# Who empties the matmul banks at the end of a batch: five copies between ScalarE and VectorE

## The chip, the cores and the metric

The kernel runs on one core of a Trainium2 chip. The metric is device time in microseconds (us) of one execution. The engines are TensorE (PE: matmuls; PEld: its weight loads), VectorE (DVE), ScalarE (ACT), GpSimd (POOL) and SyncE (SP, which here only issues transfers). Each has its own queue of instructions and works through it in order; they meet only through semaphores. TensorE writes its results to PSUM, eight banks of 128 x 512 float32; VectorE or ScalarE must read a bank before it can be used again.

## The reference

Eight batches, eight heads, 576 positions, head dimension 64, 32 memory slots. Per head an attention over compressed keys and values, then one SwiGLU feed-forward block over all heads together:

```python
a = exp(phi - max); a = a / sum(a)                     # over the 32 slots
k_m = einsum('bhsm,bhsd->bhmd', a, k)                  # 32 x 64 per head
v_m = einsum('bhsm,bhsd->bhmd', a, v)
attn = softmax(q @ k_m.T / sqrt(64))                   # 576 x 32 per head
x = (attn @ v_m), heads side by side                   # 4608 x 512
g = x @ w_gate;  val = x @ w_val                       # 512 -> 1536
out = (g * sigmoid(g) * val) @ w_out                   # 1536 -> 512
```

## The kernel before, in words

**Algebra.** `x` is never formed. For each batch the kernel multiplies the compressed values `v_m` with the gate and value weights first (`u_round`, matmuls L465). The result `t_U` has 32 rows per head, 256 rows in all, and the gates are then the product of `t_U` with the attention weights `t_A`: `p_g` for the gate, `p_v` for the value (L508), in two halves of 128 rows each. ScalarE takes silu of `p_g` (L525, into `t_sg`), VectorE multiplies it with `p_v` (L531, into `t_h`). The output product `t_h @ w_out` is done with seven block products in place of eight (Strassen's scheme in Winograd's form, `products`, matmuls L720), whose sums of blocks (`t_S`, `t_T`) are made beforehand by GpSimd and VectorE.

**Order.** Everything is in an order written out by hand. The last six batches run in one loop, `for b in range(2, B)` (L988); one pass of it is called a turn here, after its `b`. A turn begins with the scores of its batch (L389), their exponentials (L400), the sums and the normalisation of the weights (L428 to L445), mixed with the output products of the batch before. Then come 24 gate slots (`gv_slot`), and between them: the compressed keys and values of the next batch, the rest of the output products, and near slot 20 the three-part value round of the next batch, `u_three(b + 1)`. Four gate slots, 20 to 23, stand behind it, then the next turn begins.

A gate slot issues the matmuls of its own `p_g` and silu first, and then the matmuls of the `p_v` of the slot before and its multiplication. So TensorE's order at the end of a turn is: 24 small matmuls of the value round, (in turns 3, 5, 6) the last four output matmuls of the previous batch, `p_g`(20), `p_v`(19), `p_g`(21), `p_v`(20), `p_g`(22), `p_v`(21), `p_g`(23), `p_v`(22), `p_v`(23), and then the next turn's output products.

**The value round.** `u_three` fills six banks with 128 x 512 float32 each, and each is copied as bfloat16 to `t_U`. The string `evac` says by whom: one letter per bank, in order, `a` for ScalarE (L485) and `v` for VectorE (L489). "avaava" gives ScalarE the banks 1, 3, 4, 6 and VectorE 2 and 5.

**The output block.** `c21` (L772 to L776) is the last step of a batch's output product: the bank `p_os` holds the finished left half of the second row block; it is copied to `t_o2`, whose right half is already there, and the block is stored. For batches 2, 4 and 5 it is issued in turns 3, 5 and 6 directly behind the value round, at 114.7, 167.7 and 191.8 us of the profile. For the other batches it is issued elsewhere in a turn (batch 1 at 77.1, batch 3 at 132.7, batch 6 at 208.4). The last batch's is on VectorE already (`end`).

**Banks.** The eight banks are one list, first in, first out (L72 to L84):

```python
tag = free.pop(0)                      # bank(): take the first
free.append(held.pop(id(t))[0])        # done(): give back at the end
```

The list is worked through while the program is written, so which matmul gets which bank is fixed; on the chip the matmul waits until the engine that reads the bank has finished. A bank that is given back late by either engine is waited for by the matmul that stands at that place in the list, whatever other banks are free by then.

Of the kernel before, what the change touches and what calls it, by code (L numbers as in the profile page):

```python
# [14 lines left out]
def kernel(  # L15
# [59 lines left out]
    def bank(shape, dtype, name):  # L75
        tag = free.pop(0)
        t = ps.tile(shape, dtype, tag=tag, name=name)
        held[id(t)] = tag, t
        return t

    def done(*tiles):

        for t in tiles:
            free.append(held.pop(id(t))[0])  # L84
# [58 lines left out]
    def w_part(which, c, i, g, halves):  # L143

        w = W[which, c][64 * g:64 * g + 64]
        h0, h1 = halves[0], halves[-1] + 1
        return w[:, h0:h1, i] if c == 0 else w[:, i, HC * h0:HC * h1]
# [180 lines left out]
    def copy(eng, out, in_):  # L328
        if eng == "a":
            nc.scalar.copy(out=out, in_=in_)  # L330
        else:
            nc.vector.tensor_copy(out=out, in_=in_)  # L332
# [120 lines left out]
    def u_round(b, parts, evac):  # L453


        banks = []
        for which, c, halves in parts:
            w0, w1, h0, h1 = which[0], which[-1] + 1, halves[0], halves[-1] + 1
            n = (h1 - h0) * HC
            p = [bank([128, CH], FP32, f"p_u{g}") for g in range(NG)]  # L460
            for w in which:
                o = (w - w0) * n
                for i in range(NP):
                    for g in range(NG):
                        nc.tensor.matmul(  # L465
                            p[g][32 * i:32 * i + 32, o:o + n],
                            lhsT=kTs[b][64 * g:64 * g + 64, 2, 32 * i:32 * i + 32],
                            rhs=w_part(w, c, i, g, halves),
                            start=True,
                            stop=True,  # L470
                            tile_position=(64 * g, 32 * i),
                        )
            for g in range(NG):
                if (b, c, g) not in Us:
                    u_buffer(b, c, f"U{c}")
                if len(which) == 1:
                    dst = Us[b, c, g][:, h0:h1, w0]
                else:
                    dst = Us[b, c, g][:, h0]
                src = p[g][:, 0:(w1 - w0) * n].rearrange("p (a f) -> p a f", f=HC)  # L480
                banks.append((dst, src, p[g], rSs[b][:, g:g + 1] if b in scaled else None))
        for (t, p, home, r), e in zip(banks, evac):
            if e == "a":
                if r is None:
                    nc.scalar.copy(out=t, in_=p)  # L485
                else:
                    nc.scalar.activation(out=t, in_=p, func=AF.Copy, scale=r)  # L487
            elif r is None:
                nc.vector.tensor_copy(out=t, in_=p)  # L489
            else:  # L490
                nc.vector.tensor_scalar(out=t, in0=p, scalar1=r, scalar2=None, op0=ALU.mult)
            done(home)
# [51 lines left out]
    def u_buffer(b, c, tag):  # L544

        t = upool.tile([128, NG, 2, 2, HC], BF16, tag=tag, name="t_U")
        for g in range(NG):
            Us[b, c, g] = t[:, g]
# [133 lines left out]
    def products(b, by_hand, quad=None):  # L682

        h = DM // 2
        mine = {}
        lo, hi = slice(0, h), slice(h, DM)
        U = 2 if quad is None else 1
        end = quad == 1 or (quad is None and b + 1 == B)
# [65 lines left out]
        def both(name, t0, cols):  # L754
            store_block(mine[name], b, t0 // 256, cols)
# [15 lines left out]

        def c21():  # L772
            t = mine["o2"]
            copy("v" if end else "a", t[:, :, lo], mine["s"])
            done(mine["s"])
            both("o2", 256, slice(0, DM))  # L776

        def leftover(name, room, half, cols):
# [23 lines left out]
        ops = dict(  # L802
            p1=keep("p1", "s"), q6=keep("q6", "s"), p5=keep("p5", "c"),
            c11=c11, c22=c22, c12=c12, c21=c21,
        )
        if quad is not None:
# [25 lines left out]

    def u_three(b):

        u_round(b, (((0,), 0, (0, 1)), ((1,), 0, (0, 1)), ((0,), 1, (0, 1))), "avaava")

    def u_values(b):

# [119 lines left out]
    for c in range(1, NCH):  # L958
        s = 8 * c
# [28 lines left out]
    for b in range(2, B):  # L988
# [55 lines left out]
        if b == 2:  # L1044
            norm(2, 1)
            u_three(2)
            run(one[36:])
# [15 lines left out]
        if not last:  # L1063
            if b > 2:
                load_qT(b + 1)
            if b > 2 and b != 4:
                phi_sum(b + 1)
            streams += [
                (kv_items(b + 1, lambda: (u_item(b, 2, "aava")(), run(take(2)))), KV, KV + 4),
                ([lambda: (u_three(b + 1), run(take(2)))], 19, 20),  # L1070
            ]
# [38 lines left out]
```

The softmax here doesn't subtract the row's maximum and nothing guards it: scores larger than these inputs give would overflow.

## Time and profile before

| | |
|---|---|
| Time, median of 3 runs | 235.18 us (234.79 to 236.0) |
| Span of the profiled execution | 233.1 us |
| PE busy | 223.6 us, 96% |
| DVE busy | 183.2 us, 79% |
| ACT busy | 173.6 us, 74% |
| POOL busy | 140.6 us, 60% |
| ACT copies `t_U` from PSUM, L485 | 53, 607 ns each |
| DVE copies `t_U` from PSUM, L489 | 19, 683 ns each |
| ACT copies of the output block, L330 | 7, 617 ns each |
| DVE copy of the output block, L332 | 1, 692 ns |
| Ends of turns 2 to 6, us of the span | 92, 116, 145, 169, 193 |

How to read it: the clock that was granted to TensorE is full in every slice of the page. Busy time of PE counts modelled ends of pipelined matmuls, so that a row of matmuls looks gapless even where one of them started a little late; the starts tell more than the lengths. Rows of the timeline merge instructions of one kind that stand together on an engine (x4: four of them, with the time from the first start to the last end), and what is in brackets is the idle time of the engine before the row and what ended it.

### The profile page before, as it was taken

Reading aid. Unit: us, or ns where it says so; the run is one execution under the profiler, and the core shown is the slowest. Engines: PE = TensorE matmul, PEld = TensorE weight load, DVE = VectorE, ACT = ScalarE, POOL = GpSimd, SP = SyncE. Lnnn points to the kernel's source line nnn. Section 1 sums busy time; section 2 is a strip of 40 time slices with the busy share of each in tenths; the row PEclk is TensorE's granted clock in tenths of the full one; section 3 lists DMA queues with packets and bytes.
Section 4 is the critical chain, followed back from the end, with each engine's and each line's share of the span. In section 5 each row is a group of like instructions: output and inputs, shape, how many; then the busy total and the mean of one; then the engine's idle time right before and its main releaser. Section 6 shows DMA issues by size and latency. Waiting matters only on the chain.

```text
span 233.1 us, 7210 instructions
## 1 busy us (share of the span) xinstructions
PE 223.6 (96%) x2825; PEld 169.7 (73%) x2825; DVE 183.2 (79%) x421; ACT 173.6 (74%) x369; POOL 140.6 (60%) x190
## 2 busy tenths in 40 slices
PE   7987899999999999999999999999999999999993
PEld 2544466778887776878788787887788777878882
DVE  4155799999966698989798667998799888977732
ACT  2777798988447889968896658978898789677310
POOL 8422536998199059765976689464844493129291
PEclk9999999999999999999999999999999999999999
DMA  6999999999995992999099945995022702102125
GB/s 213 210 212 204 200 206 207 227 239 268 205 244 138 259 254 44 230 212 170 23 255 213 205 135 107 254 230 96 3 90 92 124 0 93 70 24 90 26 89 159
DMA packets 36674, 36.84 MB, mean 158 GB/s; under 512 B 14624, under 2 KB 31008, under 8 KB 36640
## 3 DMA queue, kind: packets, MB, share of 16 engines
q0 software_dynamic: 16272, 22.42, 51.8%
q1 hardware_dynamic: 19600, 13.18, 23.8%
q10 hardware_dynamic: 768, 0.79, 1.1%
q8 instruction: 22, 0.36, 0.6%
q14 instruction: 12, 0.10, 0.1%
HBM read 42.47 MB, written 9.44 MB: 223 GB/s over the span
## 4 chain that ended last, share of the span: by engine, by line
PE 88%; DMA 7%; POOL 1%; ACT 1%; DVE 1%; issue 1%; POOLq 0%
PE p_v L508 21%; PE p_g L508 21%; PE p_os L720 21%; PE p_oc L720 10%; DMA t_kv<-in_v_dram 7%; PE p_u L465 5%; PE p_oa L720 5%; PE p_kv L230 2%; PE p_g L389 1%; POOL t_kv L99 1%; PE p_mT L318 1%; PE p_warm L867 1%; PE p_q L376 0%; POOL t_q L108 0%; DVE t_kT L332 0%
## 5 line engine op out<-in xcount | busy, mean ns | idle before, releaser
L531 DVE TENSOR_TENSOR t_h<-t_sg,p_v 128x288 bf16<-128x288 bf16 x192 | 81.8, 451 | 17.4 <-PE p_v L508 7.4
L508 PEld LDWEIGHTS <-t_U 128*128 128x128 bf16 x768 | 73.6, 98 | 23.2 <-issue 3.8
L525 ACT ACTIVATE t_sg<-p_g 128x288 bf16<-128x288 f32 x192 | 74.0, 424 | 17.8 <-PE p_g L508 11.5
L508 PE MATMUL p_g<-t_A,t_U 128*128 128x288 bf16 x384 | 77.1, 286 | 0.5 <-ACT t_U L487 0.5
L508 PE MATMUL p_v<-t_A,t_U 128*128 128x288 bf16 x384 | 77.2, 286 | 0.0
L720 PEld LDWEIGHTS <-t_S 128*128 128x128 bf16 x384 | 37.5, 98 | 4.5 <-issue 0.2
L596 POOL TENSOR_TENSOR t_S<-t_h 128x512 bf16<-128x512 bf16 x17 | 19.6, 1154 | 32.6 <-DVE t_h L531 30.5
L720 PEld LDWEIGHTS <-t_h 128*128 128x128 bf16 x288 | 27.1, 98 | 8.6 <-issue 5.0
L485 ACT CAST t_U<-p_u 128x512 bf16<-128x512 f32 x53 | 28.0, 607 | 6.6 <-PE p_u L465 6.6
L720 PE MATMUL p_os<-t_T,t_S 128*128 128x256 bf16 x192 | 23.7, 273 | 0.0
L553 POOL TENSOR_TENSOR t_S<-t_S,t_h 128x512 bf16<-128x512 bf16 x17 | 19.6, 1154 | 1.3
L553 POOL TENSOR_TENSOR t_S<-t_h 128x512 bf16<-128x512 bf16 x16 | 18.4, 1152 | 0.0
L553 POOL TENSOR_TENSOR t_S<-t_h,t_S 128x512 bf16<-128x512 bf16 x16 | 18.4, 1150 | 0.0
L465 PE MATMUL p_u<-W,t_kT 64*32 64x512 bf16 (+1 forms) x416 | 15.8, 364 | 0.6 <-DVE t_kT L332 0.6
L720 PE MATMUL p_os<-t_T,t_h 128*128 128x256 bf16 x96 | 14.8, 273 | 0.0
L867 PE MATMUL p_warm<-bones 128*128 128x512 bf16 x44 | 13.0, 434 | 1.7 <-DVE bones L889 1.7
L489 DVE CAST t_U<-p_u 128x512 bf16<-128x512 f32 x19 | 12.4, 683 | 1.9 <-PE p_u L465 1.9
L445 DVE TENSOR_TENSOR t_A<-t_E,t_lz 128x576 bf16<-128x576 bf16 x16 | 11.4, 739 | 0.7 <-ACT t_lz L421 0.7
L720 PE MATMUL p_oc<-t_T,t_S 128*128 128x256 bf16 x96 | 11.9, 273 | 0.0
L720 PE MATMUL p_oa<-WO,t_h 128*128 128x256 bf16 x96 | 11.8, 273 | 0.0
L720 PE MATMUL p_oc<-WO,t_S 128*128 128x256 bf16 x96 | 11.8, 272 | 0.1
L720 PE MATMUL p_os<-WO,t_h 128*128 128x256 bf16 x96 | 11.8, 272 | 0.0
(106 smaller groups left out, 308.5 us busy)
## 6 DMA issues: line engine op xcount, KB each, us to landing
out_dram<-t_o SPq DMA_DIRECT2D x11, 512.0 KB, 3.5
t_kv<-in_k_dram POOLq DMA_DIRECT2D x8, 576.0 KB, 10.2
t_q<-in_q_dram POOLq DMA_DIRECT2D x8, 576.0 KB, 8.7
t_kv<-in_v_dram POOLq DMA_DIRECT2D x8, 576.0 KB, 14.8
t_phi<-in_phi_dram POOLq DMA_DIRECT2D x6, 576.0 KB, 8.1
out_dram<-t_o SPq DMA_DIRECT2D x10, 256.0 KB, 3.5
WO<-in_moe_w_out_dram POOLq DMA_DIRECT2D x3, 512.0 KB, 19.3
W<-in_moe_w_gate_dram POOLq DMA_DIRECT2D x2, 512.0 KB, 16.3
```

What stands on the lines that cost most here:

```text
L230: nc.tensor.matmul(p[g][32 * i:32 * i + 32, 0:n], lhsT=phi_of(b, g, j, i), rhs=kvs[b][64 * g:64 * g + 64, w0:w1, i, j * D:(j + 1) * D], st ...
L445: nc.vector.tensor_tensor(out=a, in0=es.pop((b, g)), in1=lzs.pop((b, g)), op=ALU.mult)
L465: nc.tensor.matmul(p[g][32 * i:32 * i + 32, o:o + n], lhsT=kTs[b][64 * g:64 * g + 64, 2, 32 * i:32 * i + 32], rhs=w_part(w, c, i, g, halve ...
L485: nc.scalar.copy(out=t, in_=p)
L489: nc.vector.tensor_copy(out=t, in_=p)
L508: nc.tensor.matmul(p[:, 0:HALF], lhsT=Us[b, c, g][:, o // 2, which, 128 * (o % 2):128 * (o % 2 + 1)], rhs=atts[b, g][:, r], start=(g == 0) ...
L525: nc.scalar.activation(out=sg, in_=gate[:, 0:HALF], func=AF.Silu)
L531: nc.vector.tensor_tensor(out=dst, in0=sg, in1=val[:, 0:HALF], op=ALU.mult)
L553: eng.tensor_tensor(out=out, in0=x, in1=y, op=ALU.subtract)
L596: eng.tensor_tensor(out=t[:, 0], in0=A21, in1=A22, op=ALU.add)
L720: nc.tensor.matmul(mine[home][:, u], lhsT=lhs(c, m, u), rhs=rhs(c, m), start=fresh and u == 0, stop=(k == 5), skip_group_check=u == 1 or n ...
L867: nc.tensor.matmul(p[:, 0:128 * a], lhsT=bones, rhs=x.to_broadcast([128, a, 128]) if a > 1 else bones, start=True, stop=True,)
```

## The change

At the end of each of the turns 2 to 6, one copy goes from ScalarE to VectorE. Its aim is to share the emptying of banks there more evenly.

- In turns 3, 5 and 6 it is the output block of the batch before (2, 4 and 5).
- In turns 2 and 4, where no output block stands there, it is the sixth copy of the value round of batches 3 and 5. The fourth and fifth change places with it, so that the two engines alternate.

```diff
         def c21():
             t = mine["o2"]
-            copy("v" if end else "a", t[:, :, lo], mine["s"])
+            copy("v" if end or b in (2, 4, 5) else "a", t[:, :, lo], mine["s"])
             done(mine["s"])
             both("o2", 256, slice(0, DM))
...
     def u_three(b):
 
-        u_round(b, (((0,), 0, (0, 1)), ((1,), 0, (0, 1)), ((0,), 1, (0, 1))), "avaava")
+        evac = "avavav" if b in (3, 5) else "avaava"
+        u_round(b, (((0,), 0, (0, 1)), ((1,), 0, (0, 1)), ((0,), 1, (0, 1))), evac)
```

The order of instructions on TensorE, GpSimd and SyncE and the order in which banks are taken and given back are the same in both kernels; VectorE has five instructions more and ScalarE five fewer.

## The prediction

> **What bounds the kernel now.** I read the busy times, then the chain of work that ended last, then who waited for whom, then the timeline at the end of a turn.
>
> The first line below is the page's busy time, the second its chain that ended last:
>
> ```profile
> PE 223.6 (96%) x2825; PEld 169.7 (73%) x2825; DVE 183.2 (79%) x421; ACT 173.6 (74%) x369; POOL 140.6 (60%) x190
> ...
> PE 88%; DMA 7%; POOL 1%; ACT 1%; DVE 1%; issue 1%; POOLq 0%
> ```
>
> TensorE (PE) is the chain; the 7% of DMA is one load before 21 us. A copy matters only where it makes a matmul start late. The 96% hides that: matmul ends are modelled, so small delays have to be read from starts. VectorE's waits give a hint where to look:
>
> ```profile
> DVE t_h L531 <- ACT t_sg L525: 5.6, 8, 0.9
> ```
>
> The eight long waits are for ScalarE gates. The five with 0.68 to 0.93 us are at the ends of turns 2 to 6. Here is the end of turn 5, like those of 3 and 6 (start, length, engine):
>
> ```profile
> 165.89 1.28 DVE L489 CAST t_U<-p_u 128x512 bf16<-128x512 f32 x2
> ...
> 166.29 1.57 ACT L485 CAST t_U<-p_u 128x512 bf16<-128x512 f32 x3
> ...
> 167.32 0.46 DVE L531 TENSOR_TENSOR t_h<-t_sg,p_v 128x288 bf16<-128x288 bf16 x1 [0.15 <-PE p_v L508]
> ...
> 167.72 0.63 ACT L330 COPY t_o<-p_os 128x512 f32<-128x512 f32 x1
> ...
> 168.03 0.41 PE L508 MATMUL p_g<-t_A,t_U 128*128 128x288 bf16 x2
> 168.20 1.38 ACT L525 ACTIVATE t_sg<-p_g 128x288 bf16<-128x288 f32 x4
> ...
> 168.41 0.72 PE L508 MATMUL p_v<-t_A,t_U 128*128 128x288 bf16 x4
> ...
> 168.70 0.82 DVE L531 TENSOR_TENSOR t_h<-t_sg,p_v 128x288 bf16<-128x288 bf16 x2 [0.93 <-ACT t_sg L525]
> ...
> 168.97 0.60 PE L720 MATMUL p_os<-WO,t_h 128*128 128x256 bf16 x4
> ```
>
> And the end of turn 4, like that of 2:
>
> ```profile
> 142.26 2.05 ACT L485 CAST t_U<-p_u 128x512 bf16<-128x512 f32 x4 [0.20 <-PE p_u L465]
> 142.33 1.28 DVE L489 CAST t_U<-p_u 128x512 bf16<-128x512 f32 x2
> ...
> 143.53 0.44 DVE L531 TENSOR_TENSOR t_h<-t_sg,p_v 128x288 bf16<-128x288 bf16 x1
> 143.55 0.41 PE L508 MATMUL p_g<-t_A,t_U 128*128 128x288 bf16 x2
> 143.87 0.41 PE L508 MATMUL p_v<-t_A,t_U 128*128 128x288 bf16 x2
> ...
> 144.17 1.37 ACT L525 ACTIVATE t_sg<-p_g 128x288 bf16<-128x288 f32 x4
> 144.36 0.72 PE L508 MATMUL p_v<-t_A,t_U 128*128 128x288 bf16 x4
> 144.66 0.82 DVE L531 TENSOR_TENSOR t_h<-t_sg,p_v 128x288 bf16<-128x288 bf16 x2 [0.69 <-ACT t_sg L525]
> ```
>
> An undisturbed pair of gate matmuls follows the one before it after 0.245 us (166.56, 166.81, 167.05, 167.30 in the same view). Against that step:
> - Turn 5: p_v after the p_g of 168.03 is due at 168.28 and starts at 168.41, 0.13 late. The next p_v (second half of the x4 row, 168.72 in the single records) is 0.07 late. Sum 0.20.
> - Turn 4: p_v is due at 143.79 and starts at 143.87, 0.08 late; the last p_v starts at 144.68, again 0.07 late. Sum 0.15.
>
> Banks are handed out first in, first out, so I can name the cause. Counting through the list in program order, the p_v of 168.41 takes the bank that the copy of the output block gives back: that copy ends at 167.72 + 0.63 = 168.36, and the matmul starts 0.05 later. The last p_v takes the bank of the first silu, which stands behind the copies: 168.20 + 0.47 = 168.67, and 0.05 later is 168.72. In turn 4 the same count gives the third ScalarE copy (end 143.82, matmul 143.87), the fourth (144.31, matmul 144.36) and the first silu (144.63, matmul 144.68). All five fit within 0.01.
>
> **What the Trainium skill says.**
> - *Perfetto Trace Analysis*, Optimization Strategy: the same gap repeating on the engine that should be saturated can mean that there is no buffer for the next tile. The trace agrees: 0.13 + 0.07 us at three ends, 0.08 + 0.07 at two, each on a bank.
> - *PSUM — Partial Sum Buffer*, Engine vs sequencer instructions: the queues of ScalarE and VectorE are strictly first in, first out. Here the silu of 168.20 had its gate product ready by 167.0 and started behind the copy.
> - The same page, Specifications (TRN2): ScalarE and VectorE can read PSUM in parallel at full bandwidth in different banks. The trace agrees: casts at 142.26 and 142.33 overlap, and VectorE's take 0.68 us each, as everywhere.
> - *VectorE: DVE Perf Modes*, the TRN2 errata: 120 cycles plus one per element from PSUM at 0.96 GHz, an estimate of 0.66 us for 512 elements; the trace has 0.683 to 0.692, which I use.
>
> **The change, part by part.** The prices (mean ns before the last bar):
>
> ```profile
> L330 ACT COPY t_o<-p_os 128x512 f32<-128x512 f32 x7 | 4.3, 617 | 3.3 <-PE p_os L720 3.3
> ...
> L332 DVE COPY t_o<-p_os 128x512 f32<-128x512 f32 x1 | 0.7, 692 | 0.6 <-PE p_os L720 0.6
> ```
>
> In a row, instructions overlap: a ScalarE copy costs a step of (2.05 - 0.62)/3 = 0.477 us, a VectorE cast 1.28 - 0.68 = 0.60, a gate multiply 0.365, a silu 0.30. Five copies move, one at each of five ends; TensorE's order is the same.
>
> *Output block to VectorE (turns 3, 5, 6; times of turn 5).* It runs after two casts: 166.49 + 0.60 = 167.09, end 167.78, its sums having ended at 166.72. Bank free at 167.83, matmul due at 168.28: 0.13 gone. The silus come 0.477 earlier, the first at 167.72, bank back at 168.25; the last p_v is now due at 168.52: 0.07 gone. Queued behind the copy on VectorE is one gate multiply, 167.32 to 167.69; its bank is back at 168.19, its user due at 168.77. The next multiplies followed the silus at 168.70 and now start near 168.23. The copy of 0.60 thus falls into the idle 0.93, and VectorE leaves the gates about 0.47 earlier, not later. TensorE gains 0.20.
>
> *Sixth copy (turns 2 and 4; times of turn 4).* "avaava" gives the fourth and sixth copy to ScalarE and the fifth to VectorE; "avavav" swaps the fourth and fifth and gives the sixth to VectorE. Fourth: VectorE, end 143.61, for the p_v due 143.79: 0.08 gone. Fifth: ScalarE, end 143.82, user due 144.04. Sixth: VectorE, 142.93 + 0.60 = 143.53, end 144.21, free 144.27, user due 144.28: met with 0.02 to spare, the one tight place. First silu: 143.69, bank back 144.20, user due 144.53: 0.07 gone. The waiting multiply goes from 143.53 to 144.13, the next to 144.49 at VectorE's own step instead of 144.66: VectorE leaves the gates 0.16 earlier. TensorE gains 0.15.
>
> *What follows.* The new turn's first gate product needs VectorE's normalisation:
>
> ```profile
> 151.95 1.39 DVE L445 TENSOR_TENSOR t_A<-t_E,t_lz 128x576 bf16<-128x576 bf16 x2
> ...
> 153.47 0.65 PE L508 MATMUL p_g<-t_A,t_U 128*128 128x288 bf16 x4
> ```
>
> The second operand is ready at 153.34 + 0.05 and used at 153.59, a margin of 0.20. VectorE is busy without a break from the last multiplies to there, so a delay would pass through; but it moves by 0.16 to 0.47 earlier and TensorE by 0.15 to 0.20. The margin stays at 0.2 and grows to 0.5. The exponentials of the scores need matmuls that end near 170.5 and have the table by 170.41 instead of 170.89: no new wait.
>
> Sum: 3 x 0.20 + 2 x 0.15 = 0.90 us. The unknown is only whether the copies keep step while TensorE writes faster: from 0.60 (the three output blocks alone) to 0.90, and more only if a wait that I don't see goes too.
>
> **The rivals.**
> 1. Forecast: 235.18 - 0.90 = 234.3, a gain of 0.38%. Chance 0.58.
> 2. Half is lost: the sixth copy misses its 0.02 or a displaced wait comes back in the later stage. 235.18 - 0.60 = 234.6. For: that margin. Against: missing it by 0.05 costs only 0.05. Chance 0.20.
> 3. ScalarE was the true limit at these ends, and the freed step returns whole: 5 x 0.477 = 2.4, so 232.8. For: ScalarE 91% busy there. Against: TensorE is late by 0.20 at most, and the rest is slack. Chance 0.07.
> 4. Nothing: TensorE catches up with a later wait (operand, bank, load) that ends at the old time. 235.2. Against: no matmul from 168.97 to the next gates is held by a wait. Chance 0.10.
> 5. Slower: VectorE, the busier of the two, doesn't absorb the copy and delays the normalisation. 5 x (0.60 - 0.20) = 2.0, so 237.2. For: the unbroken stretch. Against: idle of 0.69 to 0.93 just before it. Chance 0.05.
>
> **How the numbers follow.** The likeliest is 234.3. The bound of 0.5% is 234.0, 0.3 below the forecast and within what the runs before scatter (234.79 to 236.0), so I give it 4 in 10 of case 1, which with case 3 is 0.30 faster. Case 5 is 0.05 slower; the rest, 0.65, is within 0.5%. The range 233.6 to 235.1 takes in cases 1 and 2 with that scatter, and leaves out 3, 5 and half of 4.
>
> **What would show it.** Right: in turns 3, 5, 6 the p_v pair comes 0.245 after its p_g, the first silu directly behind the fourth cast, and VectorE's wait for a gate falls from 0.93 to below 0.1; in turns 2 and 4 three casts stand in a row on VectorE and the pairs keep 0.245. ScalarE loses about 3.0 us of busy time, VectorE gains about 3.4. Wrong: a new matmul wait for a bank of VectorE, or for the normalisation at the start of a turn.

## The result and the profile after

| | before | after |
|---|---|---|
| Median | 235.06 us (234.73 to 236.0, 6 runs) | 234.16 us (233.85 to 234.4, 6 runs) |
| Ratio | | 0.9958, 95% interval 0.9938 to 0.9977 |
| Span of the profiled execution | 233.1 us | 232.3 us |

The medians differ by 0.90 us, 0.4%, where 234.3 was forecast. A second set, beside 17 runs of the kernel before, gave 234.12 against 234.95, ratio 0.9965 (0.9952 to 0.9977). Both intervals would allow a gain of 0.54 us as well; how close to 0.90 it is must be read from the trace.

The busy times after, and VectorE's waits for gates (total, times, longest):

```profile
PE 223.0 (96%) x2825; PEld 169.8 (73%) x2825; DVE 186.2 (80%) x426; ACT 171.2 (74%) x364; POOL 140.6 (61%) x190
```

```profile
DVE t_h L531 <- ACT t_sg L525: 1.4, 3, 0.7
```

ScalarE has 2.4 us less to do and VectorE 3.0 more; of the eight waits five are gone, and the three left (at 78.2, 80.1 and 133.4 us) are not at the ends of turns. The end of turn 5 after, for the rows shown before:

```profile
165.40 2.05 ACT L485 CAST t_U<-p_u 128x512 bf16<-128x512 f32 x4 [0.20 <-PE p_u L465]
165.48 1.28 DVE L489 CAST t_U<-p_u 128x512 bf16<-128x512 f32 x2
...
166.68 0.68 DVE L332 COPY t_o<-p_os 128x512 f32<-128x512 f32 x1
...
167.27 2.08 DVE L531 TENSOR_TENSOR t_h<-t_sg,p_v 128x288 bf16<-128x288 bf16 x5
167.31 1.37 ACT L525 ACTIVATE t_sg<-p_g 128x288 bf16<-128x288 f32 x4
...
167.62 0.41 PE L508 MATMUL p_g<-t_A,t_U 128*128 128x288 bf16 x2
...
167.87 0.65 PE L508 MATMUL p_v<-t_A,t_U 128*128 128x288 bf16 x4
...
168.36 1.04 PE L720 MATMUL p_os<-WO,t_h 128*128 128x256 bf16 x8
```

The copy stands behind two casts on VectorE, 1.20 us after the first, and the silus stand directly behind the casts on ScalarE. From the last `p_g` to the output products there are now 0.74 us (three steps of 0.245), and before there were 0.94. The five multiplications are one row with no idle time in front. And the end of turn 4:

```profile
141.99 1.56 ACT L485 CAST t_U<-p_u 128x512 bf16<-128x512 f32 x3 [0.20 <-PE p_u L465]
142.07 1.88 DVE L489 CAST t_U<-p_u 128x512 bf16<-128x512 f32 x3
...
143.28 0.41 PE L508 MATMUL p_g<-t_A,t_U 128*128 128x288 bf16 x2
143.43 1.35 ACT L525 ACTIVATE t_sg<-p_g 128x288 bf16<-128x288 f32 x4
143.53 0.41 PE L508 MATMUL p_v<-t_A,t_U 128*128 128x288 bf16 x2
143.78 0.41 PE L508 MATMUL p_g<-t_A,t_U 128*128 128x288 bf16 x2
...
143.87 1.90 DVE L531 TENSOR_TENSOR t_h<-t_sg,p_v 128x288 bf16<-128x288 bf16 x5
144.02 0.65 PE L508 MATMUL p_v<-t_A,t_U 128*128 128x288 bf16 x4
```

Three casts on each engine, and every pair of gate matmuls starts 0.24 to 0.25 after the one before.

**A ruler finer than the times.** TensorE's order is the same in both kernels, so its matmuls can be paired one by one. From 29 us to the last matmul, the lead of the kernel after changes by more than 0.02 at five places and nowhere else: by 0.147, 0.198, 0.143, 0.198 and 0.196 us at the ends of turns 2 to 6. Taken from the matmul at 30.03 us of the kernel before to the last one, TensorE's stretch is 198.99 us before and 198.12 after (198.11 in the second set). What lies ahead, loads and warming up, differs by up to 0.4 between the profiled executions. I give this stretch for every experiment; it shows a tenth of a microsecond, which the times don't. It comes from one profiled execution of each kernel; where there are two or three of the same edit, they agree within 0.01.

### The profile page after: what moved, and what is told of

Its sections match the earlier page's. It is cut to its first block, busy times and chain, and to the rows that moved or that the text cites. A ratio compares the mean times of both kernels' runs of the same rounds, so it can differ in the third digit from the quotient of the medians.

```text
span 232.3 us, 7208 instructions
## 1 busy us (share of the span) xinstructions
PE 223.0 (96%) x2825; PEld 169.8 (73%) x2825; DVE 186.2 (80%) x426; ACT 171.2 (74%) x364; POOL 140.6 (61%) x190
## 4 chain that ended last, share of the span: by engine, by line
PE 86%; DMA 8%; POOL 2%; ACT 1%; issue 0%; DVE 0%; POOLq 0%
PE p_g L508 21%; PE p_os L720 21%; PE p_v L508 20%; PE p_oc L720 10%; DMA W<-in_moe_w_gate_dram 8%; PE p_u L465 6%; PE p_oa L720 5%; PE p_kv L230 2%; PE p_g L389 1%; POOL t_kv L99 1%; POOL t_kv L103 1%; PE p_q L376 0%; POOL t_q L108 0%; ACT t_qT L330 0%; PE p_kv L258 0%
## 5 line engine op out<-in xcount | busy, mean ns | idle before, releaser
L508 PEld LDWEIGHTS <-t_U 128*128 128x128 bf16 x768 | 73.6, 98 | 22.2 <-issue 3.3
L508 PE MATMUL p_g<-t_A,t_U 128*128 128x288 bf16 x384 | 77.1, 286 | 0.5 <-ACT t_U L487 0.5
L508 PE MATMUL p_v<-t_A,t_U 128*128 128x288 bf16 x384 | 76.9, 286 | 0.0
L485 ACT CAST t_U<-p_u 128x512 bf16<-128x512 f32 x51 | 27.0, 607 | 6.6 <-PE p_u L465 6.6
L489 DVE CAST t_U<-p_u 128x512 bf16<-128x512 f32 x21 | 13.6, 684 | 1.9 <-PE p_u L465 1.9
```

What stands on the lines that cost most here:

```text
L508: nc.tensor.matmul(p[:, 0:HALF], lhsT=Us[b, c, g][:, o // 2, which, 128 * (o % 2):128 * (o % 2 + 1)], rhs=atts[b, g][:, r], start=(g == 0) ...
```

## The experiments

In the recorded expectations, "bank theory" is short for the prediction's account: a `p_v` starts late because the bank that the list gives it is still being read.

| kernel | time, us | ratio to before (95%) | stretch, us | change of stretch |
|---|---|---|---|---|
| before | 235.05 | | 198.99 | |
| output block alone | 234.49 | 0.9978 (0.9971 to 0.9984) | 198.39 | -0.60 |
| value round alone | 235.08 | 1.0004 (0.9995 to 1.0013) | 198.70 | -0.29 |
| value round alone, second set | 235.2 | 1.0007 (0.9999 to 1.0016) | 198.70 | -0.29 |
| value round alone, one memset added | 235.06 | 1.0003 (0.9995 to 1.0011) | 198.70 | -0.29 |
| block on ScalarE, later | 234.49 | 0.998 (0.9971 to 0.9988) | 198.40 | -0.59 |
| one copy more on VectorE | 234.51 | 0.9981 (0.9973 to 0.9989) | 198.75 | -0.24 |
| changed kernel, second set | 234.12 | 0.9965 (0.9952 to 0.9977) | 198.11 | -0.88 |
| value round without the swap | 234.05 | 0.9965 (0.9952 to 0.9977) | 198.25 | -0.74 |
| two scalings to ScalarE | 234.13 | 0.9965 (0.9952 to 0.9977) | 198.05 | -0.94 |
| one scaling to ScalarE | 235.87 | 1.0032 (1.0019 to 1.0044) | 199.77 | +0.78 |
| two banks exchanged | 234.03 | 0.9955 (0.9943 to 0.9968) | 197.94 | -1.05 |

The kernel before had medians of 234.95 to 235.07 beside them.

**The two parts apart.** First the output block alone:

```diff
-            copy("v" if end else "a", t[:, :, lo], mine["s"])
+            copy("v" if end or b in (2, 4, 5) else "a", t[:, :, lo], mine["s"])
```

> Only the output block goes to VectorE, in turns 3, 5 and 6. Bank theory: the two late value matmuls at the ends of these turns start on time, 3 x 0.20 us earlier; at the ends of turns 2 and 4 the 0.08 and 0.07 stay. About 0.6 us below the kernel before. Rival, the copy only relieves ScalarE and each end gives back the whole step of 0.48 us: 1.4 us below. Rival, nothing is gained because a later wait takes it up: no difference.

The stretch is 0.60 shorter and the time 0.56: the bank theory's number. The whole step of 0.48 at each end (1.4) is far outside the interval.

Then the value round alone, the other half of the diff:

> Only the value round of batches 3 and 5 is shared anew, in turns 2 and 4. Bank theory: 2 x 0.15 us, about 0.3 us below the kernel before, the ends of turns 3, 5 and 6 as they were (0.13 + 0.07 late). Rival, whole step of ScalarE given back: 1.0 us below.

The stretch is 0.29 shorter, at two places, 0.15 at each. The time shows nothing, and the interval excludes the 0.3. So I ran it again, beside the changed kernel:

> The value round of batches 3 and 5 alone once more, since its trace shows the matmuls behind the two ends 0.295 us earlier and its times show nothing. If the trace tells the whole: 0.3 us below the kernel before. If something else in this kernel takes it up outside of what the profile shows: no difference again.

> The changed kernel again, beside the others on one chip and with more executions. Bank theory with both parts: 0.90 us below the kernel before (ratio 0.9962). Rival from the times of the two parts alone (0.56 and none): 0.5 us below (ratio 0.998).

The stretch was 198.70 again and the time no shorter (235.2 against 234.95, ratio 1.0007, 0.9999 to 1.0016). What hides the gain lies outside of the span: time less span (recorded to 0.1 us) is 1.73 to 1.86 us in all executions of the kernel before, with a median of 1.80 in the changed kernel, and 2.07 to 2.19 in every execution of this one. The span itself had a median 0.3 below the kernel before in the first set and 0.1 in the second. The changed kernel has both parts, without that surplus, and its 0.83 is near the sum of the stretches; it is 0.27 more than the 0.56 of the output block alone, though the intervals overlap. So for the value round the trace shows the gain, and its own times do not. One more try, with one harmless instruction added:

```diff
     nc.vector.memset(ones1, 1.0)
+    nc.vector.memset(ones1, 1.0)
```

> The value round of batches 3 and 5 alone, as in the two runs of it before, with one more instruction: a memset of the one-column tile ones1 a second time, in VectorE's idle time before 6 us. In those runs the span was 0.3 us shorter, as the bank theory has it, but the time outside of the span was 2.11 us where all executions of the kernel before have 1.73 to 1.86. If that outside part belongs to the program as loaded and not to the edit: it changes, and with 1.8 the time is 0.3 us below the kernel before. If it comes from the edit: 2.11 again and no difference in time.

The time was 235.06 against 235.07 (ratio 1.0003, 0.9995 to 1.0011), the stretch 198.70, the time outside of the span 2.08 to 2.16 as before. So one instruction more doesn't move it, and the guess that any change of the program would is not borne out. Nor does the edit alone make it, since the changed kernel contains the same edit. What does is open.

**The same gain with no copy moved.** If the order of banks is the cause, the output block can stay on ScalarE, provided that its bank is given back behind those of the last gates:

```diff
         flush_mul()
-        units, ops = products(b, ("p1", "c11"))
+        if b in (3, 5, 6):
+            ops["c21"]()
+        units, ops = products(b, ("p1", "c11", "c21") if b in (2, 4, 5) else ("p1", "c11"))
```

> No copy changes engine. In turns 3, 5 and 6 the output block stays on ScalarE but is issued behind the four last gates, so that its bank is given back behind theirs in the list. Bank theory: the p_v that took the block's bank now takes that of the first silu, which comes 0.48 us earlier; the ends of turns 3, 5, 6 lose both delays, 3 x 0.20 = 0.6 us below the kernel before, with ScalarE as busy as before. Rival, the gain is one of balance between the engines: no gain, since ScalarE has the same work.

The end of turn 5 in this kernel:

```profile
165.90 2.05 ACT L485 CAST t_U<-p_u 128x512 bf16<-128x512 f32 x4 [0.20 <-PE p_u L465]
...
167.82 1.36 ACT L525 ACTIVATE t_sg<-p_g 128x288 bf16<-128x288 f32 x4
...
168.12 0.41 PE L508 MATMUL p_g<-t_A,t_U 128*128 128x288 bf16 x2
...
168.37 0.65 PE L508 MATMUL p_v<-t_A,t_U 128*128 128x288 bf16 x4
168.85 1.47 PE L720 MATMUL p_os<-WO,t_h 128*128 128x256 bf16 x12
168.99 0.67 ACT L330 COPY t_o<-p_os 128x512 f32<-128x512 f32 x1
```

The silus are directly behind the casts, the copy behind them, and the two `p_v` pairs keep their step. The stretch is 0.59 shorter, as with the copy on VectorE, while ScalarE has all its work: it isn't the sharing of the work that brings this part, but what stands in front of the first silu and who holds which bank.

**One copy more.** In turns 3, 5 and 6 the value round is shared "avavav" too:

```diff
-        evac = "avavav" if b in (3, 5) else "avaava"
+        evac = "avavav" if b in (3, 4, 5, 6, 7) else "avaava"
```

> The changed kernel, with the sixth copy on VectorE in turns 3, 5 and 6 too (and the fourth and fifth exchanged), so that two copies leave ScalarE there. Bank theory: the output block's copy then starts behind three casts and ends at 168.38 of the time scale of turn 5, the bank comes at 168.43 where 168.28 is due: 0.15 of the 0.20 comes back as a wait for VectorE, 0.45 us above the changed kernel in all. Rival, less work on ScalarE is better: below the changed kernel, or the same.

The end of turn 3 in this kernel:

```profile
112.83 1.56 ACT L485 CAST t_U<-p_u 128x512 bf16<-128x512 f32 x3 [0.20 <-PE p_u L465]
112.93 1.89 DVE L489 CAST t_U<-p_u 128x512 bf16<-128x512 f32 x3
...
114.73 0.68 DVE L332 COPY t_o<-p_os 128x512 f32<-128x512 f32 x1
...
115.04 0.41 PE L508 MATMUL p_g<-t_A,t_U 128*128 128x288 bf16 x2
...
115.47 0.65 PE L508 MATMUL p_v<-t_A,t_U 128*128 128x288 bf16 x4
```

The copy ends at 115.41, and the `p_v` that takes its bank starts at 115.47 instead of 115.29: the wait is back, now for VectorE. The three ends lose 0.18, 0.14 and 0.14, together 0.46 where 0.45 was expected. Another 0.19 came at one output matmul near 136 us, in front of which the profile shows no wait, only "issue"; I can't explain it. The times do not show it: their median is 0.54 below the kernel before, where 0.88 less 0.46 would be 0.42 and the stretch has 0.24. Less work on ScalarE is no gain in itself.

**The same shares in another order.** The fourth and fifth copy keep their engines:

```diff
-        evac = "avavav" if b in (3, 5) else "avaava"
+        evac = "avaavv" if b in (3, 5) else "avaava"
```

> The changed kernel, but the fourth and fifth copy of the value round of batches 3 and 5 keep their engines (avaavv), so that each engine has exactly the work that it has in the changed kernel. Bank theory: the fourth copy, third on ScalarE, is still late for its p_v, so that the 0.08 us comes back at the ends of turns 2 and 4 and only the 0.07 of the last p_v is gained: 0.16 us above the changed kernel. Rival, balance alone: the same as the changed kernel, no delay at those p_v.

The end of turn 4 in this kernel:

```profile
142.19 1.56 ACT L485 CAST t_U<-p_u 128x512 bf16<-128x512 f32 x3 [0.20 <-PE p_u L465]
142.27 1.88 DVE L489 CAST t_U<-p_u 128x512 bf16<-128x512 f32 x3
...
143.49 0.41 PE L508 MATMUL p_g<-t_A,t_U 128*128 128x288 bf16 x2
...
143.81 0.41 PE L508 MATMUL p_v<-t_A,t_U 128*128 128x288 bf16 x2
```

Three casts on each engine as in the changed kernel, but the `p_v` waits for the third of ScalarE and starts 0.32 behind its `p_g` instead of 0.245. The stretch is 0.14 longer than that of the changed kernel (the two `p_v` are 0.077 and 0.079 late). The times can't tell the two apart.

**A further wait of the same kind.** In the middle of turns 2 and 4 a `p_v` of the changed kernel is 0.18 and 0.19 late. Here turn 4; L266 scales the sums of keys and values of the next batch and gives back their two banks:

```profile
130.97 0.99 DVE L266 TENSOR_SCALAR t_bkv<-p_kv,t_rS 128x128 bf16<-128x128 f32 x4
...
131.57 0.42 PE L508 MATMUL p_g<-t_A,t_U 128*128 128x288 bf16 x2
131.87 0.68 DVE L489 CAST t_U<-p_u 128x512 bf16<-128x512 f32 x1
132.02 0.42 PE L508 MATMUL p_v<-t_A,t_U 128*128 128x288 bf16 x2
```

The scalings end at 131.96 and the matmul starts 0.06 later; due was 131.82. I tried three remedies on top of the changed kernel. Their edits add lines, so that L508 is L512 in their profiles, and the casts are ScalarE's L489 and VectorE's L493. First, both scalings of the second bank on ScalarE, and "avav" for the round beside them:

```diff
-    def scaled_copy(out, p, r):
+    def scaled_copy(out, p, r, on_act=False):
+        if on_act:
+            nc.scalar.activation(out=out, in_=p, func=AF.Copy, scale=r)
+            return
...
-            scaled_copy(t[:, g].rearrange("p (a d) -> p a d", a=2), x, rSs[b][:, g:g + 1])
-            scaled_copy(t[:, 2, D * g:D * g + D], p[g][:, D:2 * D], rSs[b][:, g:g + 1])
+            on_act = g == 1 and b in (3, 5)
+            scaled_copy(t[:, g].rearrange("p (a d) -> p a d", a=2), x, rSs[b][:, g:g + 1], on_act)
+            scaled_copy(t[:, 2, D * g:D * g + D], p[g][:, D:2 * D], rSs[b][:, g:g + 1], on_act)
...
-                (kv_items(b + 1, lambda: (u_item(b, 2, "aava")(), run(take(2)))), KV, KV + 4),
+                (kv_items(b + 1, lambda: (u_item(b, 2, "avav" if b in (2, 4) else "aava")(), run(take(2)))), KV, KV + 4),
```

> The changed kernel and one more edit in turns 2 and 4: the two scalings of the second bank of the key and value sums (L266) go from VectorE to ScalarE, and the value round beside them is shared avav in place of aava. The trace shows a p_v there that starts 0.18 and 0.19 us late, 0.06 behind the last of VectorE's four scalings. Bank theory: both delays go, 0.37 us below the changed kernel. Rival: the casts behind the scalings on ScalarE start about 0.4 later and the banks that they give back are late in turn, so that half of it or all comes back.

The place in turn 4 (L267 and L269 are the scalings here):

```profile
130.87 0.54 DVE L269 TENSOR_SCALAR t_bkv<-p_kv,t_rS 128x128 bf16<-128x128 f32 x2
130.93 0.57 ACT L267 ACTIVATE t_bkv<-p_kv,t_rS 128x128 bf16<-128x128 f32 x2 [1.26 <-PE p_u L469]
...
131.47 0.42 PE L512 MATMUL p_g<-t_A,t_U 128*128 128x288 bf16 x2
131.72 0.41 PE L512 MATMUL p_v<-t_A,t_U 128*128 128x288 bf16 x2
132.03 0.41 PE L512 MATMUL p_g<-t_A,t_U 128*128 128x288 bf16 x2
```

Both `p_v` start on time (0.18 and 0.20 gained), but the stretch is only 0.06 shorter. Of what is lost again, 0.24 is the rival's case: four matmuls behind them, like the `p_g` of 132.03, start late, each 0.05 behind the end of a cast or silu on ScalarE. The other 0.11 fell at the output matmul near 136 us that was late in the kernel with one copy more; no cast, copy or silu ends in the 0.1 us in front of it, so it isn't shown to be a wait for a bank. The next expectation counts it as one. Then only the last, small scaling:

```diff
+            if g == 1 and b in (3, 5):
+                nc.scalar.activation(out=t[:, 2, D:2 * D], in_=p[g][:, D:2 * D], func=AF.Copy,
+                                     scale=rSs[b][:, g:g + 1])
+            else:
+                scaled_copy(t[:, 2, D * g:D * g + D], p[g][:, D:2 * D], rSs[b][:, g:g + 1])
```

> The changed kernel, and in turns 2 and 4 only the last of the four scalings of the key and value sums (128x64 of the second bank) goes to ScalarE; the value round beside them stays aava. With both scalings moved, the p_v started on time but 0.31 of the 0.37 us came back as waits for banks behind the casts. Bank theory: VectorE ends its third scaling 0.19 earlier than the fourth, which is what that p_v was late by, and ScalarE's casts start only about 0.25 later: 0.37 us below the changed kernel if no bank is late in turn, and between 0 and 0.37 where some are. Rival: any displacement of ScalarE's casts there costs what it brings: the same as the changed kernel.

This is slower than the kernel before. The same place of turn 4 in its timeline says why:

```profile
132.06 0.80 DVE L266 TENSOR_SCALAR t_bkv<-p_kv,t_rS 128x128 bf16<-128x128 f32 x3
...
132.89 0.31 ACT L275 ACTIVATE t_bkv<-p_kv,t_rS 128x64 bf16<-128x64 f32 x1 [2.04 <-DVE t_bkv L266]
133.11 1.55 ACT L489 CAST t_U<-p_u 128x512 bf16<-128x512 f32 x3
133.26 0.41 PE L512 MATMUL p_v<-t_A,t_U 128*128 128x288 bf16 x2 [0.18 <-ACT t_bkv L275]
```

ScalarE's scaling reads the bank that VectorE's third scaling reads as well, and waits for that one to end: 2.04 us of idle time. With both scalings of that bank on ScalarE, two engines read two different banks and started 0.06 apart (130.87 and 130.93 above), although they write parts of the same `t_bkv`. The three casts behind it in the queue, which need nothing of it, start 1.05 us behind the first scaling (in the changed kernel both start at 130.97), and every bank that they give back is late. I had reckoned the scaling's own duration and not what it waits for.

Third, no instruction changed, two places in the list of banks exchanged:

```diff
+            second = held[id(p[1])][0]
             kv_norm(b, p)
             if beside and not behind:
                 beside()
+                i = free.index(second)
+                if b in (3, 5):
+                    free[i], free[i + 1] = free[i + 1], free[i]
```

> The changed kernel, no instruction moved or changed: in turns 2 and 4 the second bank of the key and value sums and the first bank of the value round beside them change places in the list of free banks. The p_v that was 0.18 and 0.19 us late then takes a bank that is back 0.35 us sooner, and starts on time. Bank theory, counting the list on: the next users find the third cast of the round (VectorE) 0.11 late in turn 2, and the first silu behind three casts and the output block on ScalarE 0.09 late in turn 4, so that some 0.07 + 0.10 of the 0.37 stays: 0.17 us below the changed kernel by the trace, at the edge of what the times can tell. Rival, the order in the list doesn't matter: the same starts as in the changed kernel.

The same place of turn 4 in this kernel:

```profile
131.69 0.42 PE L512 MATMUL p_g<-t_A,t_U 128*128 128x288 bf16 x2
131.94 0.41 PE L512 MATMUL p_v<-t_A,t_U 128*128 128x288 bf16 x2
```

The `p_v` follows its `p_g` after 0.25. The stretch is 0.17 shorter than that of the changed kernel, the number counted. Behind it, 0.12 is lost in turn 2 and 0.10 in turn 4 at matmuls that start 0.05 behind a cast or a silu, near the 0.11 and 0.09 expected, and 0.04 at the output matmul near 136 us, which the count had not. With 234.03 us this is the fastest kernel here, though its interval (0.9943 to 0.9968) overlaps that of the changed kernel.

## Why the prediction was right, point by point

- **What bounds the kernel.** TensorE, and within it starts that wait for banks. Shown: all of the gain lies at the matmuls named; with the same shares in another order half of the gain at two ends is lost; with the output block still on ScalarE the gain at three ends is there; and exchanging two places of the list moves starts with no work changed.
- **The sizes.** Forecast 0.20 at three ends and 0.15 at two; measured 0.198, 0.198, 0.196 and 0.147, 0.143. Apart, the parts give 0.60 and 0.29 in the stretch. That the medians differ by the very 0.90 is in part luck: the stretch gave 0.87 and 0.88, the second set of times 0.83.
- **The output block on VectorE.** Forecast 1.20 us behind the first cast, and the first silu 1.91 behind ScalarE's first: 165.48 to 166.68 and 165.40 to 167.31.
- **The sixth copy.** The tight place with 0.02 to spare held: 144.02 is 143.78 plus the usual step. That the swap of the fourth and fifth is needed was in the working, and the kernel without it showed its 0.08.
- **VectorE absorbs the copies.** The idle time in front of the multiplications is gone and nothing later waits for it. How near the edge is, the kernel with one copy more shows: 0.14 to 0.18 of the 0.20 came back at each of three ends.
- **Rivals.** "The freed step returns whole" fell with the block alone (0.56, not 1.4) and with one copy more. "Slower" and "nothing" fell with the result. Of "half is lost" there is no sign in the trace; the intervals of the times alone would leave room for it.
- **Less exact.** Busy times moved by 2.4 and 3.0 us instead of 3.0 and 3.4: instructions in a row overlap, and busy time counts the overlap once (five steps of 0.477 and of 0.60 are 2.4 and 3.0). And I took the time to follow TensorE. It did for the whole change, while the value round alone gained 0.29 in the stretch and nothing in the time. Nothing in the prediction told which of the two kernels would have the surplus outside of the span; that the changed one does not was luck.

## What to carry to other kernels

When buffers go round in a fixed order, a bank given back late holds up one certain matmul even where other banks are free: count through the list, and compare the end of the copy with the start of that matmul. The remedy may be another engine, but also the place of the copy in its queue or of the bank in the list, which add no work to any engine. Before an instruction is moved to the head of another queue, ask what it waits for, since everything behind it will wait too.

## What the hardware showed that I had not expected

- From the end of a read to the start of the matmul that waits for its bank it is 0.050 to 0.052 us behind ScalarE and 0.053 to 0.059 behind VectorE at the late matmuls of these traces, steady enough to tell in most cases which of several reads a matmul waited for.
- Time less span isn't the same for all programs: medians of 1.77 to 1.80 us for seven of the kernels here, 1.89 and 1.92 for two, and 2.11 to 2.13 in three sets of the value round alone, with and without the added memset, hardly varying within a set. What sets it is open. With differences below half a microsecond it has to be looked at separately.
- One output matmul near 136 us is on time in the kernels before and after, and 0.19, 0.11 and 0.04 us late in three of the others, with no cast, copy or silu ending in the 0.1 us in front of it. That is open too: not every late start here is a wait for a bank.
